# Q and K of groups two to five sent through DRAM by chunk in a fixed order, and group four's attention one pair of expert steps earlier

## The chip, the cores and the metric

The kernel runs on one core of a Trainium2 chip. The metric is the device time of one execution in microseconds; lower is better. The core has five engines with instruction streams of their own: TensorE (PE in the profile, with its weight loads as PEld), VectorE (DVE), ScalarE (ACT), GpSimd (POOL) and SyncE (SP). Nearly all transfers are issued by SP, one behind the other; an issue that waits for something holds everything that stands behind it on SP.

## The reference

The first part is a linear attention with a complex decay for each token and channel; the second is a mixture of four dense experts on its output. Cut to what matters:

```
mag = sqrt(a_re**2 + a_im**2);  scale = min(mag, 0.999) / (mag + 1e-6)
for t in range(768):                       # for 4 batches x 8 heads, head size 48
    S = a[t] * scale[t] * S  (complex, per row)  + k[t] v[t]^T (real part)
    y[t] = q[t] @ real(S)
x = y as (3072 tokens, 384)
p = domain_probs / (sum + 1e-9)
out = sum over 4 experts e of  p[:, e] * (relu(x @ w1[e]) @ w2[e])     # 384 -> 1024 -> 384
```

Inputs and output are float32.

## The kernel before, in words

**Tiling.** The 3072 tokens are cut into 12 groups of 256 tokens (g = 0 to 11); three groups make a batch. A group has two chunks of 128 tokens (c = 0 and 1). The 384 channels are three blocks of 128 (j).

**Attention of a group.** The time loop is replaced by products within a group. For a group, `norm` (L312) scales the decays, and `prefix` (L349) forms their running products A along time on VectorE. `finish` (L390) gives two functions: `head` (L415) forms Q as A times q (L425, two instructions, real and imaginary part) and adds the group's last decays as column 128 of chunk 1 (L430, ScalarE); `tail` (L435) forms K as k divided by A (L439 to L443: three products for a factor u, then K itself in two instructions, real and imaginary part). Both have channels on the partitions. The score products need the 48 channels of one head on 48 neighbouring partitions, so Q and K are regrouped by a trip through DRAM. `trip` (L449) sends a tile out (`q_d<-Q`, `k_d<-K`; one transfer for the real and one for the imaginary part) and gives a function `back` that brings it back in the other order (`Qst<-q_d`, `Kst<-k_d`, again two transfers). `chunk` (L474) then holds the five steps of a chunk on TensorE: `turned` (K transposed, `ktp`), `increment` (what the chunk adds to the state, `dp`), `scores` (`sc`, sixteen matrix products with Kst and Qst, masked by VectorE into `scs`), and `values` (`yp`, from state and scores). `attention` (L608) runs them for groups 2 to 11 in three pieces: chunk 0 up to its scores; chunk 0's values and chunk 1's scores; chunk 1's values, the store of the output y to DRAM, for groups from 3 on its reload as `xa` (L157), and the state for the next group. Groups 0 and 1 use `near_attention` (L573).

**Experts.** Matrix products run on numbers split into a high and a low part (three products for one). Experts 0 and 1 run group by group during the attention: `moe1(g - 1)` (L628) has eight pairs k = 0 to 7 of steps, each eighteen products into `ph` (L179) and twelve into `po` (L198). Experts 2 and 3 run afterwards on blocks of 512 tokens (L829 and L842), with no attention beside them.

**What sets the order.** Before each pair, `between(k)` (L783) runs. From pair `FIRST[g]` on it hands out the three pieces of group g's attention, one per pair. It also draws on `stream` (L745), which emits the groups' preparation (`front`, L666: prefix, head, Q's trip, tail, K's trip; then the next group's norm) by a budget of microseconds per pair (`STEP`, `MORE`, against the costs that `front` yields). A `yield None` is a hold: nothing further of that group is emitted before the third piece of the previous group's attention has been handed out (`over`). For groups in `HALF` the tail and K's trip are done by chunk; for the others in one piece. After a group's last return the loads of the next group's q and k (`qk<-qkP`) and of the decays after that (`A<-aP`) are issued.

This is the order in which the program is written. A planner in the compiler then lays out each engine's instructions, and SP's issues, by its own estimates of when each is ready, with the program's order as priority; on the chip each engine runs its list strictly in that order. `behind(a, b)` (L109) makes the planner put a behind b on their engine, without a wait of its own.

Of the kernel before, what the change touches and what calls it, by code (L numbers as in the profile page):

```python
# [19 lines left out]
P = 128  # L20
# [3 lines left out]
CG = G // C  # L24
# [32 lines left out]
WARM = {6: "pq", 7: "tk", 8: "tk1"}  # L57
NSEL = 2
XSEL = 3
FIRST = {1: 5, 2: 5, 3: 4, 4: 4, 5: 3}  # L60
STEP = {1: 4.2, 2: 4.2, 3: 4.2, 4: 4.2, 5: 4.2}
MORE = (1.9, 1.9, 0.5)
HALF = (2, 3)
HOFF = 96
WIDE = 32 + P + 48
DMA_SCRATCH = 4096
# [2 lines left out]
def fast_path(ctx, tc, qkP, aP, vP, probsP, w, out, flag):  # L69
    nc = tc.nc  # L70
# [38 lines left out]
    def behind(ins, prev):  # L109
        tc.add_manual_dep(ins.ins, prev.ins.name,  # L110
                          mybir.DependencyInfo(mybir.DependencyClass.NoSync, mybir.DependencyReason.DATA),
                          reason="issue order")
# [116 lines left out]
    with ExitStack() as c1:  # L229
# [20 lines left out]
        Qst = big.tile([M, H, CG, C + 1], F32, name="Qst")  # L250
        Kst = big.tile([M, H, CG, C], F32, name="Kst")
# [97 lines left out]
        def prefix(g, A, cuts=(1, NS)):  # L349
            for i in range(1, SEG):  # L350
                x = A[:, :, i, :]
                z = tmp(f"pf{g}_{i}").rearrange("p c n -> p (c n)")[:, :4 * MS].rearrange(
                    "p (c d m) -> p c d m", c=2, d=2)
                nc.vector.tensor_tensor(z, x.unsqueeze(2).broadcast_to([P, 2, 2, MS]), bc2(A[:, :, i - 1, :]),
                                        op=ALU.mult)
                nc.vector.tensor_tensor(x[:, 0], z[:, 0, 0], z[:, 1, 1], op=ALU.subtract)
                nc.vector.tensor_tensor(x[:, 1], z[:, 1, 0], z[:, 0, 1], op=ALU.add)
                yield 1.07
            Al = A[:, :, SEG - 1, :]
            As = A.rearrange("p c i (j s) -> p c i j s", j=NJ)  # L360
            k = 1
            for lo, hi in zip(cuts, cuts[1:]):
                while k < hi:
                    nb = MS // (2 * k)
                    Ak = Al.rearrange("p c (b s) -> p c b s", s=2 * k)
                    br, bi = (Ak[:, c, :, k - 1:k].broadcast_to([P, nb, k]) for c in range(2))
                    cmul(Ak[:, :, :, k:], br, bi, [nb, k], f"sk{g}_{k}")
                    yield 0.9
                    k *= 2
                shape = [SEG - 1, NJ, hi - lo]  # L370
                br, bi = (As[:, c, SEG - 1:, :, lo - 1:hi - 1].broadcast_to([P] + shape) for c in range(2))
                cmul(As[:, :, :SEG - 1, :, lo:hi], br, bi, shape, f"fm{g}_{lo}")
                yield 0
# [72 lines left out]

            return Q, K, head, tail

        def trip(nm, X, dst, lo=0, hi=CG):  # L449
            w = X.shape[-1] if hi == CG else C  # L450
            dt = dram.tile([2, HD, hi - lo, w], F32, name=nm)
            for c in range(2):
                nc.sync.dma_start(dt[c].rearrange("(j p) n t -> p j n t", p=P),
                                  X[:, c].rearrange("p (j n) t -> p j n t", n=CG)[:, :, lo:hi, :w])

            def back():
                for c in range(2):
                    landed = nc.sync.dma_start(dst[c * IM:c * IM + D, :, lo:hi, :w],
                                               dt[c].rearrange("(h d) n t -> d h n t", d=D))
                return landed  # L460
            return back

        def t_factors(g):
# [109 lines left out]
        def near_attention(g, QK):  # L573
            Q, K = QK
            y = small.tile([M, HP, G], F32, tag="y", name=f"y{g}")
            (turn0, back0, inc0, sc0, val0), (turn1, back1, inc1, sc1, val1) = (chunk(g, c, K, y) for c in range(CG))
            if g == 0:
                state["pq"] = pick(g, "q", Q, Qst, 0, C)
                yield
            else:  # L580
                yield trip(f"q_d{g}_0", Q, Qst, 0, 1)()
                yield trip(f"q_d{g}_1", Q, Qst, 1)()
            state["tk"] = turn0()
            state["bk"] = back0()
            inc0()
            sc0()
            yield
            if g == 0:
                yield trip(f"q_d{g}", Q, Qst, 1)()
            state["tk1"] = turn1()  # L590
            back1()
            val0()
            sc1()
            xs = [turn_x(g, 0, y)]
            val1()
            xs.append(turn_x(g, 1, y))
            yield xs
            store_y(g, y)
            t_factors(g)
            inc1()  # L600
            rotate(g)
# [6 lines left out]
        def attention(g, QK):  # L608
            y = small.tile([M, HP, G], F32, tag="y", name=f"y{g}")
            (turn0, _, inc0, sc0, val0), (turn1, _, inc1, sc1, val1) = (chunk(g, c, QK[1], y) for c in range(CG))  # L610
            turn0()
            inc0()
            yield sc0()
            val0()
            t_factors(g)
            xs = [turn_x(g, 0, y)] if g < XSEL else None
            yield sc1()
            val1()
            if g < XSEL:
                xs.append(turn_x(g, 1, y))  # L620
            store_y(g, y)
            x = xs or load_x(g)
            turn1()
            inc1()
            rotate(g)
            yield x
# [37 lines left out]
        todo, last = {}, {}  # L664

        def front(g, A, qk):  # L666
            pre = prefix(g, A, cuts if g < NSEL else (1, NS))
            Q, K, head, tail = finish(g, A, qk)

            def ahead():  # L670
                for r in pre:
                    if r == 0:
                        return
                    yield r

            if g < NSEL:
                pieces = near_attention(g, (Q, K))
                yield from ahead()
                yield 1.8
                head(0, 1)  # L680
                yield 1.6
                if g == 0:
                    next(pieces)
                    tail(0, 1)
                    next(pieces)
                else:
                    next(pieces)
                yield from ahead()
                yield 2.0
                last["act"] = head(1, CG)  # L690
                yield 1.6
                last["q"] = next(pieces)
                if g > 0:
                    tail(0, 1)
                    yield 2.7
                last["dve"] = tail(1, CG)
                yield 2.7
                todo[g] = pieces
                return
            yield from ahead()  # L700
            yield 3.9
            last["act"] = head(0, CG)
            yield 3.0
            yield None
            qb = trip(f"q_d{g}", Q, Qst)
            if g in HALF:
                kb = []
                for c in range(CG):
                    last["dve"] = tail(c, c + 1)
                    yield 2.7  # L710
                    kb.append(trip(f"k_d{g}_{c}", K[0], Kst, c, c + 1))
                    if c == 0:
                        qb()
                for back in kb:
                    last["q"] = back()
            else:
                last["dve"] = tail(0, CG)
                yield 4.8
                kb = trip(f"k_d{g}", K[0], Kst)
                qb()  # L720
                last["q"] = kb()
            todo[g] = attention(g, (Q, K))

        x = {}
        for _ in front(0, A[0], qk):
            pass
# [18 lines left out]
        def stream():  # L745
            for g in range(1, NG):
                qk = load_qk(g, last["q"])
                if g + 1 < NG:
                    A.append(load_a(g + 1, prev=last["q"]))
                for r in front(g, A[g], qk):  # L750
                    yield g, r
                if g + 1 < NG:
                    for r in norm(g + 1, A[g + 1]):
                        yield g, r
# [22 lines left out]
        for g in range(1, NG + 1):  # L777
            if g == NG:
                check_all()
            first = FIRST.get(g, 2)  # L780
            end = first + len(MORE) - 1
# [24 lines left out]
    with ExitStack() as c2:  # L806
# [51 lines left out]
        for r in range(NT // T2):  # L858
            xh, xl = load_x2(r)
            prev = [fin.tile([P, C2, HD], F32, name=f"prev{e}") for e in range(E1)]  # L860
# [209 lines left out]
```

## Time and profile before

| | |
|---|---|
| median of 3 runs | 1017.98 us (1017.27 to 1019.0) |
| the profiled execution | 1022.1 us |
| its span, first to last instruction | 1020.4 us |
| mean granted TensorE clock | 0.990 |
| TensorE busy | 986.4 us, 97% |
| VectorE busy | 590.3 us, 58% |
| ScalarE busy | 363.6 us, 36% |
| SP's transfers | 94.53 MB, 32.8% of 16 engines' span |

The profile is of one execution. Times inside it run from the span's start. Up to about 57 us the first group's attention is prepared; from there to about 609 us experts 0 and 1 run with the attention of the later groups between them; after that come experts 2 and 3. A row of the timeline has the start, the duration, the engine and line, the operation, output and inputs, their shapes, how many instructions were merged (x), and in brackets how long the engine stood idle before and what ended that. Buffer numbers are left out of names, so groups are told apart by time: group two's first scores are at 137 us, group four's at 229, group five's at 272.

### The profile page before, as it was taken

What the parts mean: (1) busy time and instruction counts of PE and PEld (TensorE: products, weight loads), DVE (VectorE), ACT (ScalarE), POOL (GpSimd) and SP (SyncE); (2) the same over time, 40 slices, a digit from 0 to 9 for tenths busy, and PEclk for the clock granted to TensorE, in tenths of its full rate; (3) what the DMA queues carried; (4) which work ended last, traced back from release to release, by engine and by line L of the source; (5) the groups of instructions that cost most, each with busy time, mean ns of one, the idle gap of its engine ahead of it and who ended that gap; (6) DMA issues with size and microseconds to landing.
All of it is one profiled execution on the core that took longest, in us unless ns stands there. A gap on an engine that the chain in (4) does not pass through costs nothing.

```text
span 1020.4 us, 16210 instructions
## 1 busy us (share of the span) xinstructions
PE 986.4 (97%) x6624; PEld 926.0 (91%) x6624; DVE 590.3 (58%) x1219; ACT 363.6 (36%) x653; POOL 34.2 (3%) x64
## 2 busy tenths in 40 slices
PE   4899999999999999999999999999999999999996
PEld 2799989999899999999999999989999899989996
DVE  7798969897888989878852273232232222321221
ACT  7756526455263643626332343111111211111110
POOL 5020000000000000000000000000000000000000
PEclk9899989999999999999999999999999999999999
DMA  9474355473755738366270691021030010100001
GB/s 320 144 148 148 85 149 135 153 196 96 176 141 143 180 117 213 105 160 170 72 179 24 213 331 67 1 72 53 1 124 1 31 62 1 63 1 1 31 1 35
DMA packets 78932, 110.78 MB, mean 109 GB/s; under 512 B 5440, under 2 KB 63344, under 8 KB 78848
## 3 DMA queue, kind: packets, MB, share of 16 engines
q1 hardware_dynamic: 74560, 94.53, 32.8%
q0 software_dynamic: 4288, 15.13, 4.9%
q8 instruction: 54, 0.88, 0.4%
q14 instruction: 30, 0.25, 0.1%
HBM read 73.71 MB, written 35.92 MB: 107 GB/s over the span
## 4 chain that ended last, share of the span: by engine, by line
PE 83%; DMA 6%; DVE 5%; ACT 3%; POOL 1%; issue 1%; SPq 0%; DVEq 0%; ACTq 0%; POOLq 0%
PE pob L842 20%; PE phb L829 20%; PE ph L179 16%; PE po L198 15%; PE sc L519 5%; PE dp L507 2%; PE yp L538 2%; PE yp L533 2%; DMA Kst<-k_d 1%; DMA y_d<-y 1%; DMA xa<-y_d 1%; PE ktp L489 1%; DMA k_d<-K 1%; PE xp L569 1%; DMA q_d<-Q 1%
## 5 line engine op out<-in xcount | busy, mean ns | idle before, releaser
L835 DVE SCALAR_TENSOR_TENSOR hlb<-phb,hhb 128x512 fp32r<-128x512 f32 x96 | 66.3, 691 | 270.2 <-ACT hhb L834 270.2
L834 ACT ACTIVATE hhb<-phb 128x512 fp32r<-128x512 f32 x96 | 57.3, 597 | 314.3 <-PE phb L829 299.0
L198 PE MATMUL po<-whi,hh 128*128 128x384 f32 x384 | 129.2, 339 | 0.7 <-ACT hh L188 0.7
L842 PE MATMUL pob<-wlo,hhb 128*128 128x384 f32 x384 | 129.2, 337 | 0.0
L198 PE MATMUL po<-wlo,hh 128*128 128x384 f32 x384 | 128.9, 336 | 0.0
L842 PE MATMUL pob<-whi,hhb 128*128 128x384 f32 x384 | 128.9, 336 | 0.0
L198 PE MATMUL po<-whi,hl 128*128 128x384 f32 x384 | 123.6, 338 | 0.4 <-DVE hl L189 0.2
L842 PE MATMUL pob<-whi,hlb 128*128 128x384 f32 x384 | 120.4, 336 | 0.0
L188 ACT ACTIVATE hh<-ph 128x512 fp32r<-128x512 f32 x96 | 57.0, 595 | 159.7 <-PE ph L179 158.2
L179 PE MATMUL ph<-xha,whi 128*128 128x256 f32 x576 | 104.1, 287 | 0.9 <-ACT xha L166 0.8
L179 PE MATMUL ph<-xha,wlo 128*128 128x256 f32 x576 | 102.3, 284 | 0.0
L179 PE MATMUL ph<-xla,whi 128*128 128x256 f32 x576 | 101.7, 285 | 0.0
L189 DVE SCALAR_TENSOR_TENSOR hl<-ph,hh 128x512 fp32r<-128x512 f32 x96 | 65.9, 687 | 54.0 <-ACT hh L188 53.5
L829 PE MATMUL phb<-xhb,whi 128*128 128x512 f32 x288 | 91.8, 392 | 0.0
L179 PEld LDWEIGHTS ph<-xha,whi 128*128 128x128 f32 x576 | 85.8, 190 | 2.7 <-ACT xha L166 1.3
L179 PEld LDWEIGHTS ph<-xla,whi 128*128 128x128 f32 x576 | 83.2, 192 | 0.4 <-DVE xla L168 0.2
L179 PEld LDWEIGHTS ph<-xha,wlo 128*128 128x128 f32 x576 | 83.3, 191 | 0.2 <-issue 0.2
L829 PE MATMUL phb<-xlb,whi 128*128 128x512 f32 x288 | 82.7, 392 | 0.0
L829 PE MATMUL phb<-xhb,wlo 128*128 128x512 f32 x288 | 82.3, 393 | 0.0
L842 PEld LDWEIGHTS pob<-whi,hhb 128*128 128x128 f32 x384 | 72.1, 188 | 3.7
L842 PEld LDWEIGHTS pob<-wlo,hhb 128*128 128x128 f32 x384 | 72.1, 188 | 3.3
L198 PEld LDWEIGHTS po<-whi,hh 128*128 128x128 f32 x384 | 72.5, 189 | 1.3 <-ACT hh L188 0.9
(165 smaller groups left out, 1575.4 us busy)
## 6 DMA issues: line engine op xcount, KB each, us to landing
wst<-w SPq DMA_DIRECT2D x25, 384.0 KB, 5.8
qk<-qkP SPq DMA_DIRECT2D x24, 384.0 KB, 6.8
acc_d<-acc POOLq DMA_DIRECT2D x24, 384.0 KB, 3.8
prev<-acc_d SPq DMA_DIRECT2D x24, 384.0 KB, 4.4
A<-aP SPq DMA_DIRECT2D x22, 384.0 KB, 7.9
q_d<-Q SPq DMA_DIRECT2D x20, 387.0 KB, 4.3
Qst<-q_d SPq DMA_DIRECT2D x20, 387.0 KB, 5.5
k_d<-K SPq DMA_DIRECT2D x16, 384.0 KB, 2.9
```

The source lines that it names most:

```text
L179: ins = nc.tensor.matmul(ph[:, u, :], wt[:, j * P:(j + 1) * P], xt[:, j, :], start=(n == 0), stop=(n == 3 * NJ - 1))
L188: wts["hh"] = nc.scalar.activation(hh, ph, AF.Relu)
L189: nc.vector.scalar_tensor_tensor(hl, ph, 0.0, hh, op0=ALU.max, op1=ALU.subtract)
L198: nc.tensor.matmul(po[t], ht[:, u, t * P:(t + 1) * P], wt[:, HD:], start=(i % FE == 0 and n == 0), stop=(i % FE == FE - 1 and n == 2))
L507: nc.tensor.matmul(d_ps[:, h, :], KT[:, h, :], vc[:, h * D:(h + 1) * D], start=True, stop=True)
L519: nc.tensor.matmul(s_ps[:, h, :], Kc[:, hf * 4 + h, :], Qc[:, hf * 4 + h, :], start=True, stop=True)
L533: ins = nc.tensor.matmul(yo, st[:, o:o + n], Qc[:, o // D, :], start=True, stop=False)
L538: ins = nc.tensor.matmul(yo, vc[:, o:o + n], sc[h // 4][:, h % 4, :], start=first, stop=True)
L829: nc.tensor.matmul(ph, wt[:, j * P:(j + 1) * P], xt[:, j, :], start=(n == 0), stop=(n == 3 * NJ - 1))
L834: nc.scalar.activation(hh, ph, AF.Relu)
L835: nc.vector.scalar_tensor_tensor(hl, ph, 0.0, hh, op0=ALU.max, op1=ALU.subtract)
L842: ins = nc.tensor.matmul(po[t], ht[:, t * P:(t + 1) * P], wt[:, HD:], start=(i % FE == 0 and n == 0), stop=(i % FE == FE - 1 and n == 2))
```

## The change

Three things change, for groups 2 to 5.

- `HALF` grows from groups 2 and 3 to groups 2 to 5: their tail and K's trip are done by chunk. Two whole transfers out and two back become four and four of half the size.
- For groups in `HALF`, Q's trip goes by chunk too, and its sends are emitted ahead of the hold, where before the whole trip stood behind it. The order on SP is fixed with `behind`: sends of Q's chunks 0 and 1, return of Q's chunk 0, send of K's chunk 0, send of K's chunk 1, return of K's chunk 0, return of Q's chunk 1, return of K's chunk 1.
- `FIRST` of group 4 goes from 4 to 3: its attention's three pieces are handed out one pair earlier in the steps of `moe1(3)`, and so is the release of group 5's hold.

For groups from 6 on, the sends of Q are still whole, but are emitted in a branch of their own, ahead of the hold.

```diff
-FIRST = {1: 5, 2: 5, 3: 4, 4: 4, 5: 3}
+FIRST = {1: 5, 2: 5, 3: 4, 4: 3, 5: 3}
...
-HALF = (2, 3)
+HALF = (2, 3, 4, 5)
...
-        def trip(nm, X, dst, lo=0, hi=CG):
+        def trip(nm, X, dst, lo=0, hi=CG, prev=None):
             w = X.shape[-1] if hi == CG else C
             dt = dram.tile([2, HD, hi - lo, w], F32, name=nm)
             for c in range(2):
-                nc.sync.dma_start(dt[c].rearrange("(j p) n t -> p j n t", p=P),
-                                  X[:, c].rearrange("p (j n) t -> p j n t", n=CG)[:, :, lo:hi, :w])
-
-            def back():
+                sent = nc.sync.dma_start(dt[c].rearrange("(j p) n t -> p j n t", p=P),
+                                         X[:, c].rearrange("p (j n) t -> p j n t", n=CG)[:, :, lo:hi, :w])
+                if prev is not None:
+                    behind(sent, prev)
+
+            def back(prev=None):
                 for c in range(2):
                     landed = nc.sync.dma_start(dst[c * IM:c * IM + D, :, lo:hi, :w],
                                                dt[c].rearrange("(h d) n t -> d h n t", d=D))
+                    if prev is not None:
+                        behind(landed, prev)
                 return landed
+            back.sent = sent
             return back
...
             last["act"] = head(0, CG)
             yield 3.0
-            yield None
-            qb = trip(f"q_d{g}", Q, Qst)
             if g in HALF:
+                qb = [trip(f"q_d{g}_{c}", Q, Qst, c, c + 1) for c in range(CG)]
+                yield None
+                landed = qb[0](qb[1].sent)
                 kb = []
                 for c in range(CG):
                     last["dve"] = tail(c, c + 1)
                     yield 2.7
-                    kb.append(trip(f"k_d{g}_{c}", K[0], Kst, c, c + 1))
-                    if c == 0:
-                        qb()
-                for back in kb:
-                    last["q"] = back()
+                    kb.append(trip(f"k_d{g}_{c}", K[0], Kst, c, c + 1, landed if c == 0 else kb[0].sent))
+                landed = kb[0](kb[1].sent)
+                landed = qb[1](landed)
+                last["q"] = kb[1](landed)
             else:
+                qb = trip(f"q_d{g}", Q, Qst)
+                yield None
                 last["dve"] = tail(0, CG)
                 yield 4.8
                 kb = trip(f"k_d{g}", K[0], Kst)
```

## The prediction

> **What bounds the kernel now.** I read the page first, then the waits of TensorE, then its instructions in order of time around each wait, then the clock, then the queue that issues the transfers.
>
> ```profile
> span 1020.4 us, 16210 instructions
> PE 986.4 (97%) x6624; PEld 926.0 (91%) x6624; DVE 590.3 (58%) x1219; ACT 363.6 (36%) x653; POOL 34.2 (3%) x64
> PEclk9899989999999999999999999999999999999999
> ```
>
> TensorE is busy 97% of the span, so the change can save only its 34 us of idle time and the time at a lower clock. The clock row has two digits under 9: slice 1 counted from 0 (26 to 51 us, the start-up) and slice 5 (128 to 153 us). The waits of TensorE, taken from 57 us on, where the first groups are over:
>
> ```profile
> PE sc L519 <- DMA Kst<-k_d: 4.3, 2, 2.3
> PE sc L519 <- issue: 0.9, 1, 0.9
> PE ph L179 <- ACT xha L166: 0.8, 1, 0.8
> ```
>
> Two waits carry nearly all of it, both for K's return from DRAM before a group's first scores. In order of time, TensorE, group two (137 us), group four (229), group five (272), group six (314):
>
> ```profile
> 133.39 1.68 PE L507 MATMUL dp<-v,KT 128*112 128x48 f32 x16
> 137.08 3.78 PE L519 MATMUL sc<-Qst,Kst 112*128 112x128 f32 x16 [2.01 <-DMA Kst<-k_d]
> 227.59 1.68 PE L507 MATMUL dp<-v,KT 128*112 128x48 f32 x16
> 229.10 2.02 PE L519 MATMUL sc<-Qst,Kst 112*128 112x128 f32 x16
> 268.17 1.68 PE L507 MATMUL dp<-v,KT 128*112 128x48 f32 x16
> 272.14 3.17 PE L519 MATMUL sc<-Qst,Kst 112*128 112x128 f32 x16 [2.29 <-DMA Kst<-k_d]
> 314.75 2.02 PE L519 MATMUL sc<-Qst,Kst 112*128 112x128 f32 x16 [0.89 <-issue]
> ```
>
> The same sixteen score products take 2.02 us in groups four and six, and 3.78 and 3.17 us after the two long waits. The clock tells why (busy time by engine, then the granted clock, the DMA share and GB/s):
>
> ```profile
> 136.31:139.72 3.41, 2.64 (x12) 2.64 (x13) 0.53 (x1) 0.00 (x0) 0.00 (x0) 0.50 0.77 205
> 139.72:143.13 3.41, 3.41 (x18) 2.86 (x17) 2.64 (x8) 0.00 (x0) 0.00 (x0) 0.50 0.84 321
> 272.84:276.25 3.41, 3.41 (x18) 3.41 (x17) 1.92 (x5) 0.26 (x1) 0.00 (x0) 0.50 0.62 239
> 313.80:317.21 3.41, 2.52 (x22) 2.49 (x22) 1.29 (x4) 0.41 (x1) 0.00 (x0) 1.00 1.01 377
> ```
>
> After a wait of 2.01 us the clock was at half for 6.82 us, after 2.29 us for 3.41 us; after 0.89 us it stayed at 1.00. At half clock, half of that time is lost. In group two 3.41 - 2.64 = 0.77 us of it still belong to the wait, so half of 6.05 us is lost: the wait costs 2.01 + 3.03 = 5.04 us. Group five's costs 2.29 + 3.41/2 = 4.00 us.
>
> **The change part by part.**
>
> *K of group five by chunk.* Its trip now, on the queue that issues it (SP), and the product before it on VectorE:
>
> ```profile
> 260.63 1.82 DVE L443 TENSOR_TENSOR K<-A,u 128x768 f32<-128x768 f32 x2
> 261.61 1.32 SPq L453 DMA_DIRECT2D k_d<-K x2
> 264.29 1.33 SPq L458 DMA_DIRECT2D Kst<-k_d x2
> ```
>
> K is finished at 262.45 and has returned at 272.14: 9.7 us. For whole and half trips the trace has medians (KB each, us from issue to landing), and the longest return of a half in group two:
>
> ```profile
> k_d<-K SPq DMA_DIRECT2D x16, 384.0 KB, 2.9
> Kst<-k_d SPq DMA_DIRECT2D x16, 384.0 KB, 5.8
> k_d<-K SPq DMA_DIRECT2D x8, 192.0 KB, 4.5
> Kst<-k_d SPq DMA_DIRECT2D x8, 192.0 KB, 3.3
> DMA to landing us min/median/max: 3.0/3.6/5.8
> ```
>
> The new order is: send chunk 0, send chunk 1, return chunk 0. So the return that the scores need is issued behind a send that waits for the last product of K. How group two, which already goes by chunk, spends that time:
>
> ```profile
> 118.92 1.20 SPq L453 DMA_DIRECT2D q_d<-Q  x2
> 121.94 1.90 SPq L458 DMA_DIRECT2D Qst<-q_d  x2
> 125.29 1.04 SPq L453 DMA_DIRECT2D k_d<-K  x2
> 129.80 0.32 SPq L458 DMA_DIRECT2D Kst<-k_d  x1
> 130.21 1.00 SPq L453 DMA_DIRECT2D k_d<-K  x2
> 131.26 5.23 SPq L458 DMA_DIRECT2D Kst<-k_d  x3
> 124.71 1.02 DVE L443 TENSOR_TENSOR K<-A,u 128x384 f32<-128x384 f32 x2
> 126.52 1.02 DVE L443 TENSOR_TENSOR K<-A,u 128x384 f32<-128x384 f32 x2
> ```
>
> Lower bound: the two sends take 1.00 us of SP, two returns 0.32 x 2 plus gaps, about 0.84 us (an estimate from these rows), and the return lands in 3.3: 5.1 us after K's last product. Upper bound: chunk 0 is finished 1.81 us before chunk 1 (126.52 - 124.71), its second send is issued about 0.5 us after its product and takes 4.5 us to land, so the return starts 3.2 us after the last product; with 0.84 and 3.3 that is 7.3 us. I take 5.1, since Q's chunk 1, which lay in front of the send in group two (121.94, whole), is now returned behind K's chunk 0. Ten half products replace five whole ones: two halves take 1.02 us where one took 0.95 (1.82 for two, overlapping), so 0.07 x 5 = 0.35 us later. K's chunk 0 lands at 262.45 + 0.35 + 5.1 = 267.9 (to 270.1). TensorE is ready for it at 268.17 + 1.68 = 269.85. The wait of 2.29 us goes, or shrinks to 0.3 us, below the 0.89 us that left the clock alone. **Term: -4.00 us** (bounds -4.0 and -3.7).
>
> *Q of groups two and three by chunk.* Group two's first scores need Q and K of chunk 0. K's last product ends at 127.54; plus 5.1 us is 132.6, plus 7.3 is 134.8. TensorE is ready at 133.39 + 1.68 = 135.07. Only with the longest half return (5.8 in place of 3.3) would chunk 0 land late, at 135.1 to 137.3. The mechanism here is order: the second half of chunk 0's return is issued after 131.26 because the sends of chunk 1 (130.21) and the first return's wait stand ahead of it, and Q's whole return fills the rings while K's first send goes out. **Term: -5.04 us** (bounds 0 and -5.04; I take the full value since both 132.6 and 134.8 lie before 135.07 and the longest return alone behind it).
>
> *Group four a pair sooner.* A pair of the expert's steps, from the chain of waits:
>
> ```profile
> 299.40 2.08 PE po L198 x12
> 301.48 2.15 PE ph L179 x18
> ```
>
> That is 4.23 us. Group four's scores would be reached at 227.59 + 1.68 - 4.23 = 225.0. Its K now, last product and return:
>
> ```profile
> 216.34 1.82 DVE L443 TENSOR_TENSOR K<-A,u 128x768 f32<-128x768 f32 x2
> L458 SPq DMA_DIRECT2D Kst<-k_d x2: 320/320/321, 219.9 to 221.0; - x2
> DMA to landing us min/median/max: 4.7/5.3/5.9
> ```
>
> As it stands K would land at 221.0 + 5.9 = 226.9, which is 1.9 us too late. By chunk it lands at 218.16 + 0.35 + 5.1 = 223.6 (to 225.8): in time, or 0.8 us late without a loss of clock. In return, group four's output is stored and reloaded a pair sooner, and group five's K may start a pair sooner, which only adds slack to the first term. **Term: 0** (bounds 0 and +0.8).
>
> *What is added.* Groups two and three issue 4 more transfers each, four and five 8 each: 24 on SP, about 0.45 us each by the rows above (1.00 to 1.04 for two sends, 0.32 for a return), 11 us of SP in all. SP stands idle for K's products there (121.94 to 125.29 in group two), and that cover hides them; where it ends, K's later chunk, Q's later chunk and then the next group's qk and A loads are later by up to 3.6 us in groups four and five. The scores of chunk 1 come a pair or more behind those of chunk 0, and the next group's loads are wanted only at its own Q and K products. VectorE gains 2 x 0.35 = 0.7 us; it has room (next fence). Q's sends are moved ahead of the hold on the previous group's attention, so past that group's store and reload of y on SP. Queue order there follows readiness, and I cost it at nothing; without that cover see the rivals. **Term: 0.**
>
> **Sum:** -4.00 - 5.04 = -9.0 us. The span of 1020.4 becomes 1011.4; the profiled execution took 1022.1 us around it, the median of the runs is 1017.98. I carry the saving over to the median: **1009.0 us**.
>
> The Trainium skill has a rule on this, in "TensorE: Matmul & The Clock Gate", section "Why this matters for your kernels": idle gaps up to about 3 us do not drop the clock. The half-clock rows at 136.31 and 272.84 behind gaps of 2.01 and 2.29 us speak against it. It is the rival below that takes no clock.
>
> **The rivals.**
> 1. *One wait stays.* Group two already goes by chunk and still waits 2.01 us; if its returns keep taking 5.8 us, its 5.0 us stay: 1017.98 - 4.0 = 1014.0. Against it: Q's return in front is halved.
> 2. *VectorE hands it back.* If TensorE runs 5 us ahead after group two and VectorE doesn't follow, group four's scores are reached at 220.0 while K lands at 223.6: a wait of 3.6 plus up to 3.4 of clock, 7.0 back: 1016.0. For it: VectorE's load there. Against it: VectorE idles in group two for the same late scores, so it moves too.
>
> ```profile
> 140.00:160.00 20.00, 20.00 (x167) 18.31 (x166) 15.99 (x46) 4.11 (x10) 0.00 (x0) 0.92 0.22 76
> 220.00:240.00 20.00, 20.00 (x171) 19.22 (x170) 18.32 (x53) 5.82 (x13) 0.54 (x1) 1.00 0.59 158
> ```
>
> 3. *The clock doesn't count.* If the half clock had other causes than the waits, only 2.01 + 2.29 = 4.3 us go: 1013.7. Against it: both dips begin within such a wait or right behind it. By the rule of the page named above it would come out so.
> 4. *It does nothing.* The planner puts the scores on TensorE where it expects K; if it expects the smaller transfer sooner by as much as it is, the waits stay: 1018.
> 5. *Slower.* The first half's return stands behind the second half's send, so halving shortens nothing (group two is the evidence). Then groups two and five wait as before, and group four, a pair sooner, finds K at 226.9 in place of 225.0: 1.9 us and 1.7 to 3.4 us of clock, 1021.6 to 1023.3, about 1022.5. It decides once group four's chunk 0 returns later than about 226.
>
> **How the numbers follow.** Forecast 0.49; rival 1 0.14; rival 2 0.08; rival 3 0.03; rival 4 0.10; rival 5 0.16. A measurement tells about 0.2% (2 us) from no change. Faster: forecast, rivals 1 and 3 and half of 2, 0.70. Same: rival 4 and the other half of 2, 0.14. Slower 0.16. The forecast's own range is 1006.5 (small waits such as group six's go too) to 1011. The range over the cases is 1005.5 to 1019.0; it leaves out rival 5.
>
> **What would show it.** Right: no wait of the scores for K above 1 us at groups two and five; granted clock 1.00 from 60 us to the end; K's products 128x768 in 12 rows and 128x384 in 8 more; on SP in groups two to five the order two sends of K's chunk 0, two of chunk 1, then returns. Wrong: half-clock windows elsewhere, first scores of group four behind a wait above 1 us, or a wait for the reloaded y at the start of a group's expert steps, because Q's sends stand ahead of it on SP.

## The result and the profile after

The changed kernel takes 1013.11 us (median of 8 runs, 1011.7 to 1015.8). The kernel before, run in turn with it, takes 1019.61 us (8 runs, 1017.3 to 1023.1). The ratio is 0.9937, with a 95% interval of 0.9917 to 0.9956: 6.4 us faster, between 4.5 and 8.5.

The forecast was 9.0 us faster: 1009.0 us from a median of 1017.98. The sign is right and the size is too large. From the profile's page of the kernel after, its span, the engines' busy time and the granted clock by slice:

```profile
span 1009.9 us, 16264 instructions
PE 979.9 (97%) x6624; PEld 921.2 (91%) x6624; DVE 590.5 (58%) x1229; ACT 364.2 (36%) x653; POOL 34.2 (3%) x64
PEclk9899999999999999999999999999999999999999
```

The profiled execution took 1011.7 us around this span, so the two profiled spans differ by 10.5 us, more than the medians do. The page before had TensorE busy for 986.4 us of 1020.4, this one for 979.9 of 1009.9. So 6.5 us came out of busy time and 4.0 us out of idle time (34.0 to 30.0). The same 6624 matrix products take less busy time mainly because fewer run at half clock: the digit 8 at slice 5 of the clock row is gone. Half of the TensorE work that lies in stretches at half clock adds up to 7.28 us before, 2.55 of it in the start-up, and 2.00 after, all in the start-up. That is 5.3 of the 6.5 us; the other 1.2 are not traced.

The waits of TensorE after, from 57 to 600 us (engine, tile and line, what it waited for; us in all, times, longest):

```profile
PE sc L524 <- issue: 1.5, 2, 0.9
PE ph L179 <- ACT xha L166: 0.8, 1, 0.8
PE xp L574 <- ACT y L550: 0.7, 1, 0.7
PE po L198 <- DVE hl L189: 0.6, 1, 0.6
```

The 4.3 us of waits for K's return that stood at the top before are gone. Two waits before scores are left, 0.64 us in group two and 0.86 in group six, which the profile puts down to "issue" (nothing that it shows). Both still end 0.09 us after K's chunk 0 lands (135.20 and 306.37 us), so they are waits for K's return as well. TensorE after, in order of time, at the first scores of group two (135 us), group four (219), group five (264) and group six (306):

```profile
135.29 2.02 PE L524 MATMUL sc<-Qst,Kst 112*128 112x128 f32 x16 [0.64 <-issue]
...
218.94 2.02 PE L524 MATMUL sc<-Qst,Kst 112*128 112x128 f32 x16
...
263.62 2.02 PE L524 MATMUL sc<-Qst,Kst 112*128 112x128 f32 x16
...
306.46 2.02 PE L524 MATMUL sc<-Qst,Kst 112*128 112x128 f32 x16 [0.86 <-issue]
```

Group five no longer waits. Group two still waits 0.64 us of its 2.01. All four groups run their sixteen score products in 2.02 us, as a full clock gives them. The clock behind group two's wait (window; us, then busy time of PE, PEld, DVE, ACT and POOL with counts, granted clock, DMA share, GB/s):

```profile
135.24:138.66 3.42, 3.37 (x28) 3.11 (x29) 2.50 (x8) 0.00 (x0) 0.00 (x0) 1.00 1.15 239
```

It is at 1.00, and group six's score products at 2.02 us show no half clock either. To see where along the span the time was saved, compare the first product of an expert block behind each group's scores. Of the kernel before:

```profile
162.35 0.61 PE L179 MATMUL ph<-xha,whi 128*128 128x256 f32 x3 [0.80 <-ACT xha L166]
253.02 0.52 PE L179 MATMUL ph<-xha,whi 128*128 128x256 f32 x3
301.32 0.52 PE L179 MATMUL ph<-xha,whi 128*128 128x256 f32 x3
```

And of the kernel after:

```profile
157.81 0.62 PE L179 MATMUL ph<-xha,whi 128*128 128x256 f32 x3 [0.80 <-ACT xha L166]
248.74 0.52 PE L179 MATMUL ph<-xha,whi 128*128 128x256 f32 x3
292.65 0.52 PE L179 MATMUL ph<-xha,whi 128*128 128x256 f32 x3
```

It is 4.5 us ahead behind group two (0.5 of them were there before group two, from the start-up), 4.3 ahead at the start of the next stretch, and 8.7 ahead behind group five. So groups two and five gave about 4 us each in this pair of executions, at the places that the prediction named. The remaining 1.8 us come later, about 1.5 of them near 440 us, where two waits of TensorE, 0.72 us for `hh` of ScalarE and 0.22 for `hl` of VectorE, are absent. Of the change only the moved sends of Q reach that stretch. Yet the two waits go with the kernel and not with the execution: they stand in all five profiles with groups four and five as before, also where Q's sends are moved (e3), and in the other nine 0 to 0.7 us is left there. Why is not traced.

### The profile page after: what moved, and what is told of

Same layout as the page of the kernel before. It is cut to its first block, busy times and chain, and to the rows that moved or that the text cites. A ratio compares the mean times of both kernels' runs of the same rounds, so it can differ in the third digit from the quotient of the medians.

```text
span 1009.9 us, 16264 instructions
## 1 busy us (share of the span) xinstructions
PE 979.9 (97%) x6624; PEld 921.2 (91%) x6624; DVE 590.5 (58%) x1229; ACT 364.2 (36%) x653; POOL 34.2 (3%) x64
## 4 chain that ended last, share of the span: by engine, by line
PE 92%; DVE 2%; ACT 2%; DMA 2%; POOL 1%; issue 0%; DVEq 0%; POOLq 0%; SPq 0%
PE pob L849 20%; PE phb L836 20%; PE ph L179 20%; PE po L198 19%; PE sc L524 4%; PE dp L512 3%; PE yp L543 2%; PE yp L538 2%; PE ktp L494 1%; PE xp L574 1%; DMA mask_d<-mask 1%; DMA maskp<-mask_d 0%; PE qp L385 0%; POOL maskp L246 0%; DMA xa<-y_d 0%
```

## The transfers after

The queue that issues the transfers (SP), kernel after, group two from K's first send on (start, duration, line, tiles, transfers):

```profile
124.87 3.52 SPq L453 DMA_DIRECT2D k_d<-K  x4
128.44 1.06 SPq L460 DMA_DIRECT2D Kst<-k_d  x2
129.55 1.22 SPq L460 DMA_DIRECT2D Qst<-q_d  x2
130.82 1.74 SPq L460 DMA_DIRECT2D Kst<-k_d  x2
```

This is the order that the prediction described: K's four sends, then chunk 0's two returns. VectorE's last product of K, what chunk 0's two returns (real and imaginary part) took, and the store that GpSimd issues beside them:

```profile
126.92 1.02 DVE L443 TENSOR_TENSOR K<-A,u 128x384 f32<-128x384 f32 x2
DMA to landing us min/median/max: 3.1/4.6/6.2
128.94 0.54 POOL L638 DMA_DIRECT2D acc_d<-acc  x1 [30.86 <-ACT acc L637]
```

K is finished at 127.94, the returns are issued by 129.50, and the longest lands about 135.2: a trip of 7.26 us, where the prediction took 5.1 and had 7.3 as its upper bound. Group five, the same views:

```profile
251.67 3.77 SPq L453 DMA_DIRECT2D k_d<-K  x4
255.49 1.82 SPq L460 DMA_DIRECT2D Kst<-k_d  x2
253.97 1.02 DVE L443 TENSOR_TENSOR K<-A,u 128x384 f32<-128x384 f32 x2
DMA to landing us min/median/max: 6.6/6.6/6.6
254.30 0.54 POOL L638 DMA_DIRECT2D acc_d<-acc  x1 [20.94 <-ACT acc L637]
```

Its trip is 8.34 us, from 254.99, above the upper bound. In both groups the store of an expert's accumulator to DRAM is issued within 1.2 us of the first of the two returns. In group four no such store runs beside, and there:

```profile
L443 DVE TENSOR_TENSOR K<-A,u x4: 544/546/550, 209.9 to 212.8; 128x384 f32<-128x384 f32 x4
213.82 1.07 SPq L460 DMA_DIRECT2D Kst<-k_d  x2
DMA to landing us min/median/max: 3.5/3.8/4.1
```

K ends at 212.8 + 0.55 = 213.35 and the returns land in 3.5 to 4.1 us: about 5.2 us, the value forecast.

The new order also moved something that the prediction had left in place: the time of K's last product in group two. ScalarE's step `u<-s,lnb` (L332, of the next group's norm) starts only when the last of Q's sends has landed, 0.07 to 0.19 us behind it in all fourteen profiles. VectorE's `u<-s,u` (L338) waits for ScalarE, and it stands between K's products of chunk 0 and of chunk 1. Before, then after (ScalarE, then of the kernel after VectorE):

```profile
123.57 0.94 ACT L332 ACTIVATE u<-s,lnb 128x768 f32<-128x768 f32 x1 [0.53 <-ACT hh L188]
124.19 0.94 ACT L332 ACTIVATE u<-s,lnb 128x768 f32<-128x768 f32 x1 [1.58 <-DMA q_d<-Q]
126.04 0.96 DVE L338 TENSOR_TENSOR u<-s,u 128x768 f32<-128x768 f32 x1 [0.73 <-ACT u L337]
```

Before, Q's two whole sends take 4.58 us from the first issue to the last landing (118.92 to 123.50), and VectorE doesn't wait at L338. After, the four half sends take 5.54 us (118.47 to 124.01), and K's last product comes 0.73 us later for it.

## The experiments

The theory after this: two waits of TensorE carry the gain, with the half-clock time behind each. Group five's goes because its K comes back in halves, group two's shrinks because of the order of the transfers. The rivals: the gain comes from group four's earlier attention; or from halving alone, without the order; or group two's part is mostly chance, since the wait of one execution was taken for its usual size. "By chunk" below means sends and returns of half a K.

**Group four's attention alone, on the kernel before (e1_first_alone).**

```diff
-FIRST = {1: 5, 2: 5, 3: 4, 4: 4, 5: 3}
+FIRST = {1: 5, 2: 5, 3: 4, 4: 3, 5: 3}
```

> The kernel before with group four's attention a pair sooner and nothing else. My theory (what decides is when K's chunk 0 is back, against when TensorE reaches the first scores): group four now reaches its scores near 225 us while its whole K lands near 227, so a wait of about 2 us with half clock behind it is new, group two keeps its 2.0 us and 6.8 us of half clock, group five's K starts 1 to 2 us sooner and its wait falls from 2.3 to about 0.9 us. Ratio to before 1.000, between 0.998 and 1.003. Rival (the earlier attention is what gains, the chunks are not needed): no wait in group four, ratio 0.996 or less.

Measured: 1018.92 us, ratio 1.0004 (0.9987 to 1.0021) to the kernel before. First scores of groups two, five and six:

```profile
135.07 2.05 PE L519 MATMUL sc<-Qst,Kst 112*128 112x128 f32 x16 [0.78 <-DMA Kst<-k_d]
264.40 2.05 PE L519 MATMUL sc<-Qst,Kst 112*128 112x128 f32 x16 [0.62 <-DMA Kst<-k_d]
307.43 2.49 PE L519 MATMUL sc<-Qst,Kst 112*128 112x128 f32 x16 [3.10 <-issue]
```

The edit alone saves nothing. Group four waits 0.51 us, not the 1.9 of the prediction's slower rival. In this execution group five's wait shrank to 0.62, but group six waited 3.10 us. Group two, which the edit doesn't reach before its scores, waited 0.78 us where the first profile of before shows 2.01: the same work, another execution.

**The change without it (e2_first_back).**

```diff
-FIRST = {1: 5, 2: 5, 3: 4, 4: 3, 5: 3}
+FIRST = {1: 5, 2: 5, 3: 4, 4: 4, 5: 3}
```

> The changed kernel with group four's attention put back to where it was. My theory: chunks and order gain only about 1.4 us for K in group five, and the other 1.4 us come from the earlier attention of group four; so a wait of 0.5 to 1.2 us comes back in group five, in some executions with half clock behind it. Ratio to before 0.9945 to 0.996, that is 1 to 2 us slower than the changed kernel. Rival (chunks alone suffice): no wait in group five, ratio 0.9937 as with the whole change.

Measured: 1012.99 us, 0.9946 (0.9927 to 0.9964). Groups two, four and five don't wait, K of group five being back 1.62 us before TensorE needs it. The wait expected in group five didn't come. The runs show no worth of group four's pair in either direction: against the full change the difference is 0.9 us, plus or minus 2.7.

**By chunk in groups two and three only (e3_groups23), with group four's attention as before.**

```diff
-FIRST = {1: 5, 2: 5, 3: 4, 4: 3, 5: 3}
+FIRST = {1: 5, 2: 5, 3: 4, 4: 4, 5: 3}
...
-HALF = (2, 3, 4, 5)
+HALF = (2, 3)
```

> The changed kernel with groups four and five as before: only Q by chunk and the fixed order on SP, in groups two and three. My theory: group two's wait falls from 2.0 to about 0.6 us and its 6.8 us of half clock go, group five keeps 2.3 us and 3.4 us of half clock; span 4 us shorter than before, ratio 0.996 (0.995 to 0.997). Rival (the gain of group two came from elsewhere, or runs alike without it): ratio 0.999 to 1.001.

Measured: 1018.71 us, 1.0001 (0.9984 to 1.0018). This missed: 0.996 was expected. First scores of groups two and five:

```profile
135.47 2.02 PE L524 MATMUL sc<-Qst,Kst 112*128 112x128 f32 x16
266.22 3.32 PE L524 MATMUL sc<-Qst,Kst 112*128 112x128 f32 x16 [1.44 <-DMA Kst<-k_d]
```

The wait of group two is gone in the profile, and still the runs show no gain. Group five, whole again, waits 1.44 us and then runs at half clock.

**By chunk without the fixed order (e6_no_order).** Each send and return then stands where the planner puts it.

```diff
-                landed = qb[0](qb[1].sent)
+                landed = qb[0]()
...
-                    kb.append(trip(f"k_d{g}_{c}", K[0], Kst, c, c + 1, landed if c == 0 else kb[0].sent))
-                landed = kb[0](kb[1].sent)
-                landed = qb[1](landed)
-                last["q"] = kb[1](landed)
+                    kb.append(trip(f"k_d{g}_{c}", K[0], Kst, c, c + 1))
+                landed = kb[0]()
+                landed = qb[1]()
+                last["q"] = kb[1]()
```

> The changed kernel without the fixed order: the trips of groups two to five still go by chunk and group four is still a pair sooner, but the compiler's planner places them on SP. It puts both returns of Q ahead of K's sends, and K's chunk 0 return ahead of chunk 1's send. My theory: group two is as before the change (Q's whole return ahead of K's send), wait of 1.5 to 2 us with half clock; groups four and five have no wait, since K's first return no longer stands behind the second send. Ratio 0.998 (0.997 to 0.9995). Rival (order on SP doesn't matter, the size of the pieces does): ratio 0.9937 as with the whole change.

Measured: 1015.34 us, 0.9961 (0.9945 to 0.9977). First scores of group two:

```profile
136.66 3.65 PE L524 MATMUL sc<-Qst,Kst 112*128 112x128 f32 x16 [1.33 <-DMA Kst<-k_d]
```

Group five doesn't wait. On SP one of chunk 0's two returns now stands behind chunk 1's sends in group two, and this execution has the wait again. Halving, together with group four's pair, keeps 4.0 us of the gain, and the trips in groups four and five are even shorter (4.4 and 3.5 us). Neither the expected 0.998 nor the rival's 0.9937 came. Against the full change the difference is 2.4 us, plus or minus 2.6, so these runs alone don't show that the order counts.

**The fixed order in groups four and five only (e7_groups45);** two and three keep the steps of before.

```diff
-HALF = (2, 3, 4, 5)
+HALF = (4, 5)
+OLDH = (2, 3)
...
+            if g in OLDH:
+                yield None
+                qb = trip(f"q_d{g}", Q, Qst)
...
+                    if c == 0:
+                        qb()
```

> The changed kernel with groups two and three as they were before the change (K by chunk, Q whole, order left to the planner); groups four and five by chunk in the fixed order. The instructions of TensorE, VectorE and ScalarE stand in the same order as in the changed kernel; only SP's differ. Theory A (groups four and five carry the whole gain; group two's long wait in the profiled execution of before was not a typical one): ratio 0.9937 to 0.995. Theory B (the order in group two is worth 2 to 4 us, and the run with groups two and three alone did not show it because the waits of groups five and six came after it): ratio 0.9965 to 0.998.

Measured: 1016.35 us, 0.9971 (0.9953 to 0.9989): 3.0 us faster than before. Group two waits 1.17 us, as in the second profile of before, and group five doesn't wait. The full change is 3.5 us faster than this one, plus or minus 2.7 (the two intervals' half-widths, 0.0020 and 0.0018, as the root of the sum of squares). So group two's order does count once groups four and five are by chunk. The other kernels agree: the five more that have a fixed order in group two and group five by chunk (e2, e5, e8, e9, e10) lie at 0.992 to 0.9955, the two without the order in group two (e6 and this one) at 0.9961 and 0.9971. Alone, in e3, it did not show.

**Chunk 0's return ahead of chunk 1's send (e9_early_return).** The prediction took its lower and upper bounds from a return that stands behind the second send; this takes it out of there.

```diff
-                kb = []
-                for c in range(CG):
-                    last["dve"] = tail(c, c + 1)
-                    yield 2.7
-                    kb.append(trip(f"k_d{g}_{c}", K[0], Kst, c, c + 1, landed if c == 0 else kb[0].sent))
-                landed = kb[0](kb[1].sent)
-                landed = qb[1](landed)
-                last["q"] = kb[1](landed)
+                last["dve"] = tail(0, 1)
+                yield 2.7
+                k0 = trip(f"k_d{g}_0", K[0], Kst, 0, 1, landed)
+                landed = k0(k0.sent)
+                last["dve"] = tail(1, 2)
+                yield 2.7
+                k1 = trip(f"k_d{g}_1", K[0], Kst, 1, 2, landed)
+                landed = qb[1](k1.sent)
+                last["q"] = k1(landed)
```

> The changed kernel with one place on SP exchanged in groups two to five: K's chunk 0 is returned ahead of the send of chunk 1, no longer behind it. Theory A (the return waits on SP for the second half's product and send): from K's last product to the landing of chunk 0 it takes 4.4 to 5 us in place of 5.2 to 8.3, group two's wait falls to nothing; ratio 0.992 to 0.9935. Theory B (the transfers themselves set the time, the place on SP doesn't matter): times and waits as with the whole change, ratio 0.9937.

Measured: 1013.38 us, 0.9942 (0.9921 to 0.9963), no different from the change. SP in group two:

```profile
125.01 0.96 SPq L453 DMA_DIRECT2D k_d<-K  x2
128.61 0.86 SPq L460 DMA_DIRECT2D Kst<-k_d  x2
129.51 1.00 SPq L453 DMA_DIRECT2D k_d<-K  x2
```

The trip falls from 7.26 to 4.14 us, and K is back 1.77 us before it is needed, so group two doesn't wait. For that, chunk 1 comes later: its scores in group four wait 0.80 us. Group six waits 1.74.

**The accumulator's stores moved away (e5_acc_late).** Two stores that run beside K's returns of groups two and five are issued behind them, on SP.

```diff
+LATE = ((1, 0), (3, 1))
...
+                if (g, e) in LATE:
+                    held.append((g, e, acc))
+                    return
...
+                    while held:
+                        hg, he, acc = held.pop()
+                        behind(nc.sync.dma_start(acc_d[hg][he], acc), last["q"])
```

> The changed kernel with two of the 24 stores of the experts' partial sums (expert 0 of group one, expert 1 of group three, 384 KB each) taken from GpSimd's queue and issued on SP behind K's last return of groups two and five. In the profile of the changed kernel they run beside K's trips of these groups. Theory A (they take the transfers' time: trips of 7.3 and 8.3 us in groups two and five against 5.1 and 5.2 in three and four, which have no store beside them): the two trips fall to 5.1 to 6 us, group two's wait of 0.64 us goes, ratio 0.992 to 0.993. Theory B (the store beside them is without effect): trips of 7 to 8 us, ratio 0.9937.

Measured: 1015.32 us, 0.9955 (0.9942 to 0.9968). The trips shortened as expected, in group two from 7.26 to 5.17 us and in group five from 8.34 to 6.58. The time did not follow: there is no wait in groups two and five, but 4.6 us are saved where the change saved 6.4, the intervals overlapping. So the trips are 1.8 to 2.1 us shorter without the store beside them, one profile against one, and taking it away gains nothing that these runs can tell. In group five the store is not all: without it the two returns still took 5.1 and 5.4 us. Group six waits 1.83 us, with half clock behind it.

**Group six by chunk as well (e8_to_six).**

```diff
-HALF = (2, 3, 4, 5)
+HALF = (2, 3, 4, 5, 6)
```

> The changed kernel with group six by chunk in the fixed order too. Group six's first scores wait 0.9 to 3.1 us for its whole K in all six profiles so far, with half clock behind it in two. Theory A: that wait goes, 1 to 4 us less, ratio 0.990 to 0.9925. Theory B (the next wait takes its place, group seven or eight, whose K now lands 0.1 to 2.9 us ahead of its scores): ratio 0.9937.

Measured: 1012.66 us, 0.9933 (0.9915 to 0.9951). First scores of group two:

```profile
137.33 2.02 PE L524 MATMUL sc<-Qst,Kst 112*128 112x128 f32 x16 [2.32 <-issue]
```

Group six's wait is gone: K is back 3.8 us early. The time is that of the change within the intervals. In the same execution group two, whose steps are those of the changed kernel, waited 2.32 us, as long as in the first profile of before. So the changed order doesn't rule out group two's wait. The clock stayed at 1.00 behind it.

**The kernel before, profiled a second time (before_again), and e3 twice more (e3_again, e3_third),** none of them with a new edit, to see how far one execution's waits stand for the kernel.

> The kernel before, unchanged, for a second profile. Its first profiled execution (1022.1 us) lies at the slow end of 62 executions (1014 to 1023). Theory A (the two long waits of that profile are not typical; each varies with how K's transfers land): group two's wait 0.5 to 1.5 us, group five's 0.5 to 1.5, clock lost 2 to 5 us against 7.3, span near 1016. Theory B (typical): both waits near 2 us again, span near 1020.

> The kernel with only groups two and three in the new order, unchanged, for a second profile. In its timed runs it is no faster than before, in its first profile it was (1014.6 us span, no wait in group two). Theory A (what group two saves, groups five and six lose again, because their whole K isn't sooner): no wait in group two, 2 to 3 us in group five or six, span 1016 to 1019. Theory B (group two's wait is often there in spite of the order): a wait of 1 us or more in group two.

> As the run before it, a third profile of the same kernel: theory A no wait in group two and 2 to 3 us in groups five or six; theory B a wait of 1 us or more in group two.

One execution each: 1021.57, 1019.37 and 1016.6 us, beside 1019.89 for the kernel before (median of 11). First scores of groups two, five and six in the kernel before:

```profile
136.60 3.53 PE L519 MATMUL sc<-Qst,Kst 112*128 112x128 f32 x16 [1.18 <-DMA Kst<-k_d]
270.16 2.07 PE L519 MATMUL sc<-Qst,Kst 112*128 112x128 f32 x8 [2.31 <-DMA Kst<-k_d]
313.52 2.73 PE L519 MATMUL sc<-Qst,Kst 112*128 112x128 f32 x15 [1.68 <-issue]
```

And of e3's third execution, groups two and five:

```profile
136.15 2.02 PE L524 MATMUL sc<-Qst,Kst 112*128 112x128 f32 x16 [1.70 <-issue]
267.87 3.66 PE L524 MATMUL sc<-Qst,Kst 112*128 112x128 f32 x16 [2.11 <-DMA Kst<-k_d]
```

The second one had 0.08 us at group two and 1.79 at group five. Group two's wait goes with the execution, in the old order and in the new one. Group five's, with a whole K, is there each time.

**Early return and group six together (e10_early_six):** the edit of e9 and

```diff
-HALF = (2, 3, 4, 5)
+HALF = (2, 3, 4, 5, 6)
```

> The changed kernel with K's chunk 0 returned ahead of chunk 1's send and with group six by chunk too. Theory A (both take away waits that are left, 0.6 us of group two and 0.9 to 1.8 us of group six with its half clock): ratio 0.989 to 0.9925. Theory B (what is left is spread over waits that these don't touch): ratio 0.993 to 0.995.

Measured: 1012.12 us (6 runs, 1011.45 to 1013.24), 0.992 (0.9901 to 0.9939). First scores of groups two, five and six:

```profile
134.53 2.02 PE L524 MATMUL sc<-Qst,Kst 112*128 112x128 f32 x16
263.53 2.02 PE L524 MATMUL sc<-Qst,Kst 112*128 112x128 f32 x16
305.12 2.02 PE L524 MATMUL sc<-Qst,Kst 112*128 112x128 f32 x16
```

None of these waits; K is back 2.68, 4.78 and 5.88 us before TensorE is ready. Its runs spread over 1.8 us, the change's over 4.1. It beats the kernel before; that it beats the change isn't shown, since the intervals overlap.

The waits of all profiles side by side (us; "h" marks half-clock windows of 3.41 us behind the wait, "hh" two of them):

| kernel | group two | group five | group six |
|---|---|---|---|
| before | 2.01 hh | 2.29 h | 0.89 |
| before_again | 1.18 h | 2.31 h | 1.68 h |
| e1 | 0.78 | 0.62 | 3.10 h |
| e7 (old order in two) | 1.17 h | 0 | 1.53 h |
| e6 (no order) | 1.33 h | 0 | 1.63 h |
| e3, e3_again, e3_third | 0, 0.08, 1.70 | 1.44 h, 1.79 hh, 2.11 h | 1.21, 2.44, 0.78 |
| after | 0.64 | 0 | 0.86 |
| e2 | 0 | 0 | 0.91 |
| e8 | 2.32 | 0 | 0 |
| e5 | 0 | 0 | 1.83 h |
| e9 | 0 | 0 | 1.74 |
| e10 | 0 | 0 | 0 |

## Why the prediction was right, and where it was off

*What bounds the kernel* held: the two waits for K's return and the half clock behind them were what the change could take, and the saving lies at these two places.

*K of group five by chunk, -4.00 us: right in size, by another route.* With a whole K and the attention of before, five profiles show waits of 2.29, 1.44, 2.31, 1.79 and 2.11 us (mean 1.99), with half clock behind each; half of one 3.41-us window four times and of two once is 2.05 on average, together 4.0 us. By chunk the wait is 0 in all eight profiles. But the trip shortened only from 9.65 to 8.34 us, past the prediction's upper bound of 7.3 and not to its 5.1, with the accumulator's store beside it (6.58 without, in e5). Against the room of before, 7.40 us from K's last product to the moment at which TensorE is ready (269.85 - 262.45), 8.34 would still have left a wait of 0.9. It vanished because the room had grown to 8.8 us (263.78 - 254.99), as the prediction had said of group four's earlier attention without counting on it: the by-chunk profiles with that pair have 8.3 to 8.8, e2 without it 7.67. In e2 the trip happened to be 6.05, and that was enough. So that the term came out to the last tenth is partly luck; after has 0.46 us to spare.

*Q of groups two and three by chunk, -5.04 us: this is the step that failed, in its size,* for three reasons.

First, most of what the order gains is handed back. The order does shorten the trip from K's last product to the landing of chunk 0: 8.3 to 9.5 us in the old order (before, before_again, e1, e7; mean 8.6), 6.1 to 8.2 in the new (after, e2, e3 three times, e8; mean 6.9). But Q's four half sends need 5.5 to 6.4 us from first issue to last landing (mean 6.0), where the two whole ones needed 4.5 to 5.1 (mean 4.8). By the chain through ScalarE and VectorE shown above K's last product comes later by as much: from it to the moment at which TensorE is ready there are 7.2 to 7.5 us in the old order (mean 7.4) and 5.9 to 6.7 in the new (mean 6.2). So of 1.7 us, 1.2 are lost again. The prediction had kept K's last product at 127.54; 1.2 us later its own landings of 132.6 and 134.8 become 133.8 and 136.0, the second behind the 135.07 at which TensorE is ready.

Second, chunk 0's longer return took 6.2 us here, beside the accumulator's store. The prediction did name this case: a return of 5.8 us lands chunk 0 late.

Third, the price was the wait of one execution, 2.01 us with two half-clock windows, the dearest of all that were seen in the old order: 2.01, 1.18, 0.78 and 1.17 (mean 1.29), with 3.03, about 1.7, 0 and about 1.7 us of clock (mean 1.6). The new order had 0.64, 0, 0, 0.08, 1.70 and 2.32 (mean 0.79) without half clock. So the step saves about 0.5 + 1.6 = 2.1 us by these means. The 1.6 may be partly luck: in the new order windows with 1.22 and 1.54 us of idle time kept the full clock, in the old order windows with 1.17 and 1.18 lost it.

The sum with this term in place is -4.0 - 2.1 = -6.1 us, against -6.4 measured (-8.5 to -4.5). It is made of means of a few profiles each, so the agreement is a check and not a proof. *Carrying the sum over from the span to the median* is where the third reason entered: the profiled execution of before took 1022.1 us, 4 us above the median of its runs, and both waits were priced from it. Against its own span the change saved 10.5 us, against the median 6.4.

*Group four a pair sooner, 0: right.* e1 bounds its effect on the time to about 2 us on either side, e2 to about 3; what it gave group five's K is told above. Its scores came at 218.94, not 225.0, with K back about 0.5 us before. The prediction had left its own savings in group two out of the 225.0 (with the start-up part 4.5 us); the other 1.6 are not traced.

*The added transfers and half products, 0: right for the loads, not for the rest.* Behind the change no wait for a late load and none for the reloaded y appears in the waits of TensorE; the 0.7 and 0.8 us for `y` and `xha` lie in groups one and two, which don't reload y, and stood there before. But the added sends of Q delayed K's last product, as said. And one wait is new, 0.58 us for VectorE's `hl` at 204.99: the eight profiles with groups four and five by chunk have 0.23 to 0.94 us there, the other six at most 0.14. On average that is about as much as the missing waits near 440 us give back.

*The rivals.* One wait stays (1014.0): in part. Group two's stays in some executions (0.64, 1.70, 2.32), and the measured -6.4 lies between that rival's -4.0 and the forecast's -9.0, with neither inside the interval. VectorE hands it back: not seen, since group four's K is in time and the 4 us gained in group two are still there at 248.74. The clock doesn't count: against it stand the clock rows, and 4.7 us of the 10.5 saved were half clock in groups two and five. It does nothing, and slower: ruled out by the interval; the slower rival needed group four's chunk 0 after about 226, and it was back by 218.5.

*Left open:* group two's new order alone (e3, 0 plus or minus 1.7 us) and groups four and five alone (e7, 3.0 less) add up to 3.0 us, the whole change saves 6.4. The gap of about 3.5 is barely more than the three intervals together (3.2). e3's profiles don't explain it: group five waits 1.44, 1.79 and 2.11 us there against 2.29 and 2.31 before, and group six 1.21, 2.44 and 0.78 against 0.89 and 1.68, so what group two gains isn't seen to go to them. Nor is it settled why e5, with the shorter trips, isn't faster than the change.

## What to carry to other kernels

Price a wait from several executions where its length hangs on transfers: the profile of one run, above all one above the median of its runs, sets the term too high. When the wait is for a trip through DRAM, look first at what stands ahead of its return in the issuing queue and which other store runs beside it; moving the return ahead of the next send brought group two's trip from a mean of 6.9 us to 4.1 and 3.5 (e9, e10), as the change's own order had brought it from 8.6 to 6.9, though neither step showed in the time by itself. Ask also who waits for a transfer that is cut up: four half sends landed later than two whole ones, and through two engines that delayed the very product whose trip was to be shortened. Once the first waits are gone, look for the next of the same kind (group six here), and treat those that are usually short as well, since they are long in some executions.

## What the runs showed of the hardware

Less idle time than the prediction's 2 us can cost clock. TensorE in e7, a window with 1.17 us of idle time, and the one behind it:

```profile
133.49:136.90 3.41, 2.24 (x22) 2.12 (x22) 1.88 (x7) 0.00 (x0) 0.00 (x0) 1.00 0.51 137
136.91:140.31 3.40, 3.40 (x20) 3.14 (x18) 1.37 (x3) 0.00 (x0) 0.00 (x0) 0.50 1.05 243
```

And in e9, 1.69 us of idle time in a window:

```profile
305.84:309.24 3.40, 1.71 (x15) 1.74 (x16) 1.23 (x3) 0.48 (x1) 0.00 (x0) 1.00 1.03 332
309.25:312.66 3.41, 3.41 (x26) 3.27 (x27) 3.27 (x12) 0.00 (x0) 0.00 (x0) 1.00 0.29 108
```

Behind the first the clock fell to half, behind the second it did not. Half clock comes in whole windows of 3.41 us in these profiles; counted in steps of that length from 57 to 600 us, idle time of 1.12, 1.17, 1.18, 1.24, 1.33, 1.44, 1.53, 1.63 and 1.68 us in a window at full clock was followed by one or two windows at half, and so were all five of 1.81 us and more; 1.21, 1.22, 1.54, 1.70 and 1.74 were not, nor anything up to 1.08. So between about 1.1 and 1.8 us something else decides, which these runs don't show. The rule that the prediction took from the Trainium skill ("TensorE: Matmul & The Clock Gate", section "Why this matters for your kernels"), gaps up to about 3 us leaving the clock alone, doesn't hold in this kernel.

What a return took went with whether it was issued ahead of or behind a store from another engine's queue. In the six profiles with the new order in group two, chunk 0's second return (192 KB) is issued 0.1 to 0.5 us behind the store of a 384 KB accumulator from GpSimd's queue; it took 5.0 to 7.1 us and landed 0.9 to 2.6 us after the store. In e9 and e10, where it is issued 0.2 and 0.5 us ahead of the store (and of chunk 1's sends), it took 3.7 and 3.5 us, and in e5, without the store, 4.0. And one kernel differs between executions by more than the change saves: the kernel before took from 1014.3 to 1024.3 us over all its runs.
